# A transformer block with its gradients, rewritten: folded attention algebra, a token-major FFN in four column groups, transposes by DMA

## The chip, the core and the metric

The kernel runs on one core of a Trainium2 chip. A core has a matrix engine (TensorE, PE in the profile; loading its stationary operand is PEld), VectorE (DVE), ScalarE (ACT), GpSimd (POOL), a queue engine that only issues transfers (SP), and 16 DMA engines that all queues share. The engines run side by side and wait for each other through semaphores. The metric is the device time of one execution in microseconds, the median of several.

## The reference, cut to what matters

One block of a network with pre-layernorm, linear attention and a gated FFN, and the gradients of its output with respect to the input and the five weight matrices. S = 2048 tokens, D = 640 features, 32 heads of 20, F = 1728. Everything is bf16. `B_x` isn't used.

```python
def _A_ref(x, wqkv, wo):
    q, k, v = split_heads(x @ wqkv)
    phi = lambda t: jnp.where(t > 0, t + 1, jnp.exp(t)) + 1e-6
    pq, pk = phi(q), phi(k)
    kv = jnp.einsum("bhsd,bhse->bhde", pk, v)
    z = jnp.einsum("bhsd->bhd", pk)
    num = jnp.einsum("bhqd,bhde->bhqe", pq, kv)
    den = jnp.einsum("bhqd,bhd->bhq", pq, z)[..., None] + 1e-6
    return merge_heads(num / den) @ wo

def _B_ref(x, w_gate, w_up, w_down):
    g = _silu(x @ w_gate)
    u = x @ w_up
    return (g * u) @ w_down

h = x + _A_ref(_layernorm(x), A_wqkv, A_wo)
h2 = h + _B_ref(_layernorm(h), B_w_gate, B_w_up, B_w_down)
# outputs: h2, then the vjp of h2 at grad_out for A_x, A_wqkv, A_wo, B_w_gate, B_w_up, B_w_down
```

The attention has no softmax: all tokens share one 20x20 matrix kv per head and one vector z. In the gradients grad_out plays the part of dh2, the gradient to the FFN's input is turned into dh1 by the backward pass of the second layernorm and the residual, and dh1 goes back through the attention.

## The kernel before, in words

A matmul on TensorE contracts over the 128 partitions: `lhsT` is held still (128x128), `rhs` streams past column by column, and the result is summed in a PSUM bank of 512 fp32 columns. Which index lies on the partitions is therefore what a layout means here: token-major (`_tm`: 128 tokens on the partitions, 16 token tiles of 640 features) or feature-major (`T`: 128 features on the partitions, five tiles of 2048 tokens). A product that contracts over features needs feature-major operands, a weight gradient contracts over tokens and needs token-major ones, so most tensors are wanted in both. The kernel makes the second form on TensorE: `transpose_into` (lines 119 to 131) multiplies 128x128 blocks with an identity and copies groups of up to eight from PSUM to SBUF, by turns on VectorE (line 89) and ScalarE (line 91).

The stages, in the order of the text:

1. Lines 292 to 358. Layernorm of x (`bn_stats`, line 174; the norm, line 197), transposes to xnT, q feature-major (lines 310 to 317), k and v token-major (331 to 343), phi by exp and relu (236 to 240). grad_out is loaded and transposed (346 to 350), and so is wqkv (351 to 356).
2. Lines 363 to 415. kv as a block-diagonal matrix KVbd and its transpose, z, the denominators per token tile (389), their reciprocals spread over features by a small matmul (407), the numerators (411). The results are stored in DRAM.
3. Lines 420 to 434. Output projection plus residual (426, 428), second layernorm, transposes.
4. Lines 463 to 565, the FFN. The 1728 hidden features are cut into 14 tiles of 128 (the last has 64), in seven groups of two. Per hidden tile and chunk of 512 tokens: gate (494), up (498) and the gradient to the product, pdm = w_down dh2 (502), each five matmuls of 512 columns; ScalarE copies them out of PSUM (505 to 511) and VectorE forms m, du and dg (513 to 523). The three rows are stored feature-major in DRAM (524 to 526), transposed into token-major strips (528), and used for the gradients of w_down (552) and of w_gate and w_up (561).
5. Lines 609 to 631: h2 = h + m w_down (621), with m read back by token tile, and transposes of w_gate and w_up (599).
6. Lines 649 to 668: the gradient to the normalised h (663), and `ln_bwd_tile` (209 to 231), which gives dh1.
7. Lines 671 on: the attention backward. The gradient of wo (697), do (721), the denominators' gradient (731), dq (750), the gradients of kv (774, 779), dv and dk (803, 808), the gradient to xn and from it to x (837), the gradient of wqkv (856). Between them stand nine sets of transposes and several reloads from DRAM.

A planner places the instructions: it keeps each engine's list, takes the program's order as priority, and puts in semaphores and buffer waits. Tiles are drawn from pools; a tile with the same tag waits for a free buffer of its pool. The large tensors share a pool of six (`big`), 20 KB per partition each. SP issues most loads, POOL issues the stores and some loads, ACT a few.

Of the kernel before, what the change touches and what calls it, by code (L numbers as in the profile page):

```python
# [8 lines left out]
FP32 = mybir.dt.float32  # L9
BF16 = mybir.dt.bfloat16  # L10
ALU = mybir.AluOpType
# [5 lines left out]
DEBUG_OUT = {}  # L17
BIG_BUFS = 6
USE_BN_STATS = True
LN_MODE = "split"  # L20


class RR:

    def __init__(self, items):
        self.items = list(items)
        self.i = 0

    def __call__(self):
        it = self.items[self.i % len(self.items)]  # L30
        self.i += 1
        return it
# [3 lines left out]
def kernel(  # L36
    ctx, tc, A_x, A_wqkv, A_wo, B_x, B_w_gate, B_w_up, B_w_down, grad_out,
    out_0, out_1, out_2, out_3, out_4, out_5, out_6,
):
    nc = tc.nc  # L40
# [4 lines left out]
    SC = S // 512  # L45
    DT = D // P
    D3T = 3 * DT
    FT = (F + P - 1) // P
    fsz = [min(P, F - i * P) for i in range(FT)]
    NCH = [(i, min(i + 320, D)) for i in range(0, D, 320)]  # L50
    NW0 = NCH[0][1] - NCH[0][0]
    assert S % 512 == 0 and D % P == 0 and F % 64 == 0 and D % 320 == 0
    BIGSHAPE_TM = [P, ST, D]
    BIGSHAPE_FM = [P, DT, S]

    outs_list = [out_0, out_1, out_2, out_3, out_4, out_5, out_6]

    def dbg(name, ap, kind):
        if name not in DEBUG_OUT:
            return  # L60
        o = outs_list[DEBUG_OUT[name]]
        flat = o.rearrange("b s d -> (b s d)") if len(o.shape) == 3 else o.rearrange("a b -> (a b)")
        if kind == "tm":
            W = ap.shape[-1]
            v = flat[0:S * W].rearrange("(t p w) -> p t w", p=P, w=W)
        elif kind == "fm":
            J = ap.shape[1]
            v = flat[0:J * P * S].rearrange("(j p s) -> p j s", p=P, s=S)
# [10 lines left out]
    keep = ctx.enter_context(tc.tile_pool(name="keep", bufs=1))  # L79
    dram = ctx.enter_context(tc.tile_pool(name="dram", bufs=1, space=bass.MemoryType.DRAM))  # L80
    big = ctx.enter_context(tc.tile_pool(name="big", bufs=BIG_BUFS))

    dma_rr = RR([nc.sync, nc.gpsimd, nc.sync])
    evac_rr = RR(["v", "s"])

    def evac_copy(out, in_, eng=None):
        e = eng or evac_rr()
        if e == "v":
            nc.vector.tensor_copy(out=out, in_=in_)  # L89
        else:  # L90
            nc.scalar.copy(out=out, in_=in_)  # L91

    ident = const.tile([P, P], BF16, name="ident")
    make_identity(nc, ident[:])
    ones_bf = const.tile([P, H], BF16, name="ones_bf")
    nc.vector.memset(ones_bf[:], 1.0)
    eps6_col = const.tile([P, 1], FP32, name="eps6_col")
    nc.vector.memset(eps6_col[:], 1e-6)

    Efull = const.tile([P, D], BF16, name="Efull")  # L100
    nc.vector.memset(Efull[:], 0.0)
    E = Efull[:H, :]
    nc.gpsimd.memset(E, 1.0)
    nc.gpsimd.affine_select(out=E, in_=E, pattern=[[1, D]], compare_op=ALU.is_ge,
                            fill=0.0, base=0, channel_multiplier=-Dh)
    nc.gpsimd.affine_select(out=E, in_=E, pattern=[[-1, D]], compare_op=ALU.is_ge,
                            fill=0.0, base=Dh - 1, channel_multiplier=Dh)
    Mbd = const.tile([P, DT, D], BF16, name="Mbd")
    ET = const.tile([P, DT, H], BF16, name="ET")
# [6 lines left out]
    def tiles_overlapping(c0, c1):  # L116
        return [i for i in range(DT) if not (head_range(i)[1] <= c0 or head_range(i)[0] >= c1)]

    def transpose_into(dst_fn, src_fn, nblk, rows_in, ps_pool, tag="tr", cols_in=P, group=8, eng=None):
        b = 0  # L120
        group = max(1, min(group, (8 * P) // rows_in))
        while b < nblk:
            nb = min(group, nblk - b)
            pt = ps_pool.tile([P, 8 * P], BF16, name="pt_" + tag, tag=tag)
            for j in range(nb):
                src = src_fn(b + j)
                nc.tensor.transpose(out=pt[:cols_in, j * rows_in:(j + 1) * rows_in], in_=src,  # L127
                                    identity=ident[:rows_in, :rows_in])
            evac_copy(dst_fn(b, nb), pt[:cols_in, :nb * rows_in], eng)
            b += nb  # L130

    def tm_to_fm(dstT, src_tm, W, ps_pool, eng=None, tag="tr"):
        WT = W // P
        for j in range(WT):
            transpose_into(
                dst_fn=lambda b0, nb, j=j: dstT[:, j, b0 * P:(b0 + nb) * P],
                src_fn=lambda b, j=j: src_tm[:, b, j * P:(j + 1) * P],
                nblk=ST, rows_in=P, ps_pool=ps_pool, eng=eng, tag=tag)

    def fm_to_tm(dst_tm, srcT, W, ps_pool, eng=None, tag="tr"):  # L140
        WT = W // P
        for t in range(ST):
            transpose_into(
                dst_fn=lambda b0, nb, t=t: dst_tm[:, t, b0 * P:(b0 + nb) * P],
                src_fn=lambda b, t=t: srcT[:, b, t * P:(t + 1) * P],
                nblk=WT, rows_in=P, ps_pool=ps_pool, eng=eng, tag=tag)

    def layernorm_tiles(src_tm, dst_tm, mean, rstd, t0, nt, work, mode="bn"):
        mv = mean[:, t0:t0 + nt]
        rv = rstd[:, t0:t0 + nt]  # L150
        if mode == "act":
            ssum = work.tile([P, nt], FP32, name="ln_ssum", tag="ln_ssum")
            ssq = work.tile([P, nt], FP32, name="ln_ssq", tag="ln_ssq")
            for k in range(nt):
                t = t0 + k
                junk = work.tile([P, D], BF16, name="ln_junk", tag="ln_junk")
                nc.scalar.activation(out=junk[:], in_=src_tm[:, t, :], func=ACT.Copy, accum_out=ssum[:, k:k + 1])
                junk2 = work.tile([P, D], BF16, name="ln_junk2", tag="ln_junk")
                nc.scalar.activation(out=junk2[:], in_=src_tm[:, t, :], func=ACT.Square, accum_out=ssq[:, k:k + 1])
            nc.vector.tensor_scalar(out=mv, in0=ssum[:], scalar1=1.0 / D, scalar2=None, op0=ALU.mult)  # L160
            msq = work.tile([P, nt], FP32, name="ln_msq", tag="ln_msq")
            nc.vector.tensor_tensor(out=msq[:], in0=mv, in1=mv, op=ALU.mult)
            var = work.tile([P, nt], FP32, name="ln_var", tag="ln_var")
            nc.vector.scalar_tensor_tensor(out=var[:], in0=ssq[:], scalar=1.0 / D, in1=msq[:],
                                           op0=ALU.mult, op1=ALU.subtract)
            nc.vector.tensor_scalar(out=rv, in0=var[:], scalar1=1e-5, scalar2=None, op0=ALU.add)
        elif mode == "bn":
            a = len(NCH)
            mvv = work.tile([P, nt, 2], FP32, name="ln_mv", tag="ln_mv")
            for k in range(nt):  # L170
                t = t0 + k
                st6 = work.tile([P, a, 6], FP32, name="ln_st6", tag="ln_st6")
                for ci, (n0, n1) in enumerate(NCH):
                    nc.vector.bn_stats(out=st6[:, ci, :], in_=src_tm[:, t, n0:n1])
                nc.vector.bn_aggr(out=mvv[:, k, :], in_=st6[:].rearrange("p a b -> p (a b)"))
            nc.vector.tensor_copy(out=mv, in_=mvv[:, :, 0])
            nc.vector.tensor_scalar(out=rv, in0=mvv[:, :, 1], scalar1=1e-5, scalar2=None, op0=ALU.add)
        else:
            ssum = work.tile([P, nt], FP32, name="ln_ssum", tag="ln_ssum")
            ssq = work.tile([P, nt], FP32, name="ln_ssq", tag="ln_ssq")  # L180
            for k in range(nt):
                t = t0 + k
                nc.vector.tensor_reduce(out=ssum[:, k:k + 1], in_=src_tm[:, t, :], axis=AX.X, op=ALU.add)
                junk = work.tile([P, D], BF16, name="ln_junk", tag="ln_junk")
                nc.scalar.activation(out=junk[:], in_=src_tm[:, t, :], func=ACT.Square, accum_out=ssq[:, k:k + 1])
            nc.vector.tensor_scalar(out=mv, in0=ssum[:], scalar1=1.0 / D, scalar2=None, op0=ALU.mult)
            msq = work.tile([P, nt], FP32, name="ln_msq", tag="ln_msq")
            nc.vector.tensor_tensor(out=msq[:], in0=mv, in1=mv, op=ALU.mult)
            var = work.tile([P, nt], FP32, name="ln_var", tag="ln_var")
# [700 lines left out]
```

## Time and profile before

| | |
|---|---|
| three runs | 1111.87, 1112.3, 1115.91 us; median 1112.3 |
| the profiled execution | span 1114.9 us; no other time is given for it |
| TensorE | 1056.7 us busy, 95%, 8337 matmuls |
| VectorE, ScalarE, GpSimd | 571.8, 483.0, 133.4 us busy |
| DMA | 134.24 MB, mean 120 GB/s |
| mean granted TensorE clock | 0.981 |

How to read it: busy times are unions of the instructions' own intervals. Matmuls are pipelined, so the mean length of one (299 ns for 320 columns) is longer than the distance between two starts, and a busy PE isn't yet one at its peak. In a group's row stand the line, the engine, the operation, output and inputs by name, the shape, the count, then busy us and mean ns of one, then the idle time of the engine just ahead of it and who ended it. A DMA row ends with the size of one transfer and the median us from issue to landing.

### The profile page before, as it was taken

The numbers are of one execution on the slowest core, as the hardware profiler recorded it, in microseconds if no ns is written. First come the engines' busy times: TensorE is split into PE (matmuls) and PEld (weight loads), VectorE is DVE, ScalarE is ACT, GpSimd is POOL, SyncE is SP. The second block draws the span as 40 slices with busy tenths as digits, with TensorE's granted clock in tenths as the row PEclk, the third lists the DMA queues.
The fourth block names the chain that finished last, engine by engine and source line by source line (L and its number), as shares of the span: only waits on it lengthen the run. The fifth ranks groups of instructions, "written<-read, shape, count | busy, mean of one in ns | idle before, by whom it ended". The sixth has DMA issues, their size and how long they took to land.

```text
span 1114.9 us, 20384 instructions
## 1 busy us (share of the span) xinstructions
PE 1056.7 (95%) x8337; PEld 714.7 (64%) x8337; DVE 571.8 (51%) x1441; ACT 483.0 (43%) x951; POOL 133.4 (12%) x224
## 2 busy tenths in 40 slices
PE   5899998999999999999996999599989999899998
PEld 2477665575847576666756777377767467577775
DVE  8766676727273545545361232234343985477321
ACT  5755587526262535345351010122233686744231
POOL 2100000120202111111312013000000000011110
PEclk9899899999999999999999999799999999999999
DMA  8244364312222222212045954955440039411110
GB/s 318 75 138 150 159 247 146 125 61 86 92 82 96 78 103 78 98 41 107 31 159 182 219 136 139 298 119 122 100 153 31 1 123 351 181 39 43 42 36 30
DMA packets 134669, 134.24 MB, mean 120 GB/s; under 512 B 92384, under 2 KB 115680, under 8 KB 134320
## 3 DMA queue, kind: packets, MB, share of 16 engines
q0 software_dynamic: 20208, 77.58, 18.8%
q1 hardware_dynamic: 85440, 48.03, 15.4%
q10 hardware_dynamic: 28928, 7.34, 3.4%
q8 instruction: 65, 1.06, 0.4%
q14 instruction: 28, 0.23, 0.1%
HBM read 71.50 MB, written 61.42 MB: 119 GB/s over the span
## 4 chain that ended last, share of the span: by engine, by line
PE 69%; DMA 6%; DVE 6%; issue 1%; ACT 1%; POOL 0%; POOLq 0%; DVEq 0%; ACTq 0%; SPq 0%
PE accw L561 10%; PE acch L663 10%; PE acc_dxn L837 6%; PE accf L621 6%; PE acc_dwqkv L856 6%; PE pu L498 4%; PE pg L494 4%; PE acc L552 4%; PE pt_trs L127 4%; PE pt_tr L127 3%; PE pdm L502 3%; DMA dgcols<-scr_dgT 3%; PE acc_dwo L697 2%; PE ps_do L721 2%; DVE dm L519 1%
## 5 line engine op out<-in xcount | busy, mean ns | idle before, releaser
L561 PEld LDWEIGHTS <-hn_tm 128*128 128x128 bf16 x1120 | 107.1, 98 | 16.0 <-issue 4.8
L494 PE MATMUL pg<-hnT,wg_blk 128*128 128x512 bf16 (+1 forms) x280 | 76.2, 384 | 3.3 <-DMA wg_blk<-in_B_w_gate_dram 3.3
L663 PE MATMUL acch<-wgT,dgcols 128*128 128x320 bf16 x448 | 67.9, 304 | 12.0 <-DMA dgcols<-scr_dgT 11.5
L498 PE MATMUL pu<-hnT,wu_blk 128*128 128x512 bf16 (+1 forms) x280 | 74.7, 379 | 0.0
L89 DVE CAST dw_sb<-accw 128x256 bf16<-128x256 f32 (+1 forms) x35 | 14.5, 415 | 111.7 <-PE accw L561 86.8
L502 PE MATMUL pdm<-dh2T,wdT 128*128 128x512 bf16 (+1 forms) x280 | 69.6, 379 | 1.1 <-ACT dm L511 1.0
L552 PE MATMUL acc<-dh_tm,m_strip 128*128 128x320 bf16 (+1 forms) x448 | 69.3, 299 | 0.0
L621 PE MATMUL accf<-wd_big,mcols 128*128 128x320 bf16 x448 | 64.8, 306 | 3.6 <-DMA mcols<-scr_mT 3.6
L663 PE MATMUL acch<-wuT,ducols 128*128 128x320 bf16 x448 | 66.4, 300 | 0.0
L856 PE MATMUL acc_dwqkv<-cur_tm,xn_tmr 128*128 128x320 bf16 x480 | 65.7, 299 | 0.0
L663 PEld LDWEIGHTS <-dgcols 128*128 128x128 bf16 x448 | 44.4, 99 | 30.4 <-DMA dgcols<-scr_dgT 11.8
L561 PE MATMUL accw<-dg_strip,hn_tm 128*128 128x256 bf16 (+1 forms) x560 | 60.5, 269 | 3.4 <-ACT dw_sb L91 2.9
L561 PE MATMUL accw<-du_strip,hn_tm 128*128 128x256 bf16 (+1 forms) x560 | 60.3, 269 | 0.7 <-DVE dw_sb L89 0.7
L856 PEld LDWEIGHTS <-xn_tmr 128*128 128x128 bf16 x480 | 46.9, 98 | 18.1
L621 PEld LDWEIGHTS <-mcols 128*128 128x128 bf16 x448 | 44.0, 100 | 22.1 <-DMA mcols<-scr_mT 3.7
L91 ACT CAST dw_sb<-accw 128x256 bf16<-128x256 f32 (+1 forms) x35 | 12.8, 364 | 103.8 <-PE accw L561 98.9
L214 ACT ACTIVATE lb_dy<-acch 128x320 bf16<-128x320 f32 x32 | 14.0, 436 | 97.6 <-PE acch L663 97.6
L663 PEld LDWEIGHTS <-ducols 128*128 128x128 bf16 x448 | 44.0, 98 | 17.3
L552 PEld LDWEIGHTS <-m_strip 128*128 128x128 bf16 (+1 forms) x448 | 41.8, 99 | 13.5 <-issue 0.3
L229 DVE SCALAR_TENSOR_TENSOR lb_t<-lb_dy,lb_nm,lb_t 128x640 bf16<-128x640 bf16 x32 | 28.2, 880 | 41.1 <-ACT lb_t L227 41.1
L502 PEld LDWEIGHTS <-wdT 128*128 128x128 bf16 (+1 forms) x280 | 27.0, 98 | 34.4 <-DVE wdT L89 3.1
L565 POOL DMA_DIRECT2D out_dram<-dw_sb x70 | 37.7, 539 | 79.5 <-DVE dw_sb L89 44.9
(264 smaller groups left out, 2068.2 us busy)
## 6 DMA issues: line engine op xcount, KB each, us to landing
scr_mT<-mT_row POOLq DMA_DIRECT2D x14, 512.0 KB, 2.9
scr_duT<-duT_row POOLq DMA_DIRECT2D x14, 512.0 KB, 3.7
scr_dgT<-dgT_row POOLq DMA_DIRECT2D x14, 512.0 KB, 2.9
ducols<-scr_duT ACTq DMA_DIRECT2D x16, 448.0 KB, 4.7
mcols<-scr_mT SPq DMA_DIRECT2D x16, 448.0 KB, 4.1
dgcols<-scr_dgT SPq DMA_DIRECT2D x16, 448.0 KB, 4.2
out_dram<-dw_sb POOLq DMA_DIRECT2D x60, 64.0 KB, 1.8
x_tm<-in_A_x_dram SPq DMA_DIRECT2D x4, 640.0 KB, 6.3
```

The costliest lines, as they stand in the source:

```text
L127: nc.tensor.transpose(out=pt[:cols_in, j * rows_in:(j + 1) * rows_in], in_=src, identity=ident[:rows_in, :rows_in])
L229: nc.vector.scalar_tensor_tensor(out=t2[:], in0=dy[:], scalar=nm[:, 0:1], in1=t1[:], op0=ALU.subtract, op1=ALU.subtract)
L494: nc.tensor.matmul(pg[:fs, :], lhsT=wg_blk[:, kt, coff:coff + fs], rhs=hnT[:, kt, cs], start=(kt == 0), stop=(kt == DT - 1))
L498: nc.tensor.matmul(pu[:fs, :], lhsT=wu_blk[:, kt, coff:coff + fs], rhs=hnT[:, kt, cs], start=(kt == 0), stop=(kt == DT - 1))
L502: nc.tensor.matmul(pdm[:fs, :], lhsT=wdT_i[:, kt, :], rhs=dh2T[:, kt, cs], start=(kt == 0), stop=(kt == DT - 1))
L552: nc.tensor.matmul(acc[:fs, :w], lhsT=m_strip[:, t, coff:coff + fs], rhs=dh2_tm[:, t, n0:n1], start=(t == 0), stop=(t == ST - 1))
L561: nc.tensor.matmul(acc[:, :gw], lhsT=hn_tm[:, t, dt_ * P:(dt_ + 1) * P], rhs=strip[:, t, :gw], start=(t == 0), stop=(t == ST - 1))
L565: nc.gpsimd.dma_start(out=o_ap[dt_ * P:(dt_ + 1) * P, gcol0:gcol0 + gw], in_=dw_sb[:, :gw])
L621: nc.tensor.matmul(acc[:, :w], lhsT=mcols[:, j, :], rhs=wd_nat[:, j, n0:n1], start=(j == 0), stop=(j == FT - 1))
L663: nc.tensor.matmul(acc[:, :w], lhsT=cols[:, j, :], rhs=wT[:, j, n0:n1], start=(k == 0), stop=(k == 2 * FT - 1))
L837: nc.tensor.matmul(acc[:, :w], lhsT=srcT[:, jj, t * P:(t + 1) * P], rhs=wqkvT[:, j, n0:n1], start=(k == 0), stop=(k == D3T - 1))
L856: nc.tensor.matmul(acc[:, :w], lhsT=xn_tmr[:, t, dt_ * P:(dt_ + 1) * P], rhs=cur_tm[:, t, n0:n1], start=(t == 0), stop=(t == ST - 1))
```

## The change

The function is written anew; the reference, the inputs and the launch are the same. What it does:

**Algebra.** v, the numerators, o and do are no longer formed. With Y = xn^T pk (640x640), the matrix of all heads is kv^T = mask(wv^T Y), and W2 = kv wo; the attention's output is (pq/den) W2. Backward, dp = dh1 W2^T is the gradient to pq/den, GT = dh1^T (pq/den) stands for the gradient of wo (dwo = kv^T G) and of kv (mask(wo GT)), WV2 = dkv^T wv^T is the share of dv in the gradient to xn, and dwv = Y dkv. z is summed by a matmul with ones, which spreads it over all partitions, and the denominators are formed on VectorE.

**FFN, token-major.** Columns in four groups of 448, 448, 448 and 384. dm is computed ahead for all groups; then, per group, gate and up for two token tiles at a time, 896 wide; m, du and dg come out token-major and go into the weight gradients as they are. The gradient of w_down is formed as its transpose.

**Transposes by DMA.** Only xn is transposed on TensorE. All else uses a transposing DMA issued on SP: grad_out, the weights, pq/den, hn, every tile of dg and du (through a small tile `stg` to DRAM), m (read back from DRAM), dh1, and pk, dq and dk one tile at a time in a ring of three.

**Order.** Loops over token tiles run with a lag of one or two tiles, the down projection stands at the end, and the rstd is a power on GpSimd, not ScalarE's square root. The large pool has five buffers, a pool `strips` four.

The diff, of which the removed side is the listing above; the added side cut to its core:

```diff
+    def mm_row(ps, lhs, rhs, n, start=True, stop=True):
+        for ci, (n0, n1) in enumerate(NCH):
+            for k in range(n):
+                nc.tensor.matmul(ps[:, ci, :320], lhsT=lhs(k), rhs=rhs(k, n0, n1),
+                                 start=(start and k == 0), stop=(stop and k == n - 1))
...
+    for (t0, t1) in ((0, 1), (1, 2), (2, 4), (4, 6), (6, 8), (8, 10), (10, 12), (12, 14), (14, 16)):
...
+            tp = psum.tile([P, D], BF16, name="ps_t", tag="mm")
+            for kt in range(DT):
+                nc.tensor.transpose(tp[:, kt * P:(kt + 1) * P], xn[:, t, kt * P:(kt + 1) * P], ident[:])
+            nc.scalar.copy(out=xnT[:, :, t * P:(t + 1) * P], in_=tp[:].rearrange("p (k c) -> p k c", c=P))
+            for (dst, w0) in ((pk, D), (pqa, 0)):
+                ps = mm("ps_kq")
+                mm_row(ps, lambda k: xnT[:, k, t * P:(t + 1) * P], lambda k, n0, n1: wqk[:, k, w0 + n0:w0 + n1], DT)
+                nc.scalar.activation(out=e[:, :, :320], in_=row(ps), func=ACT.Exp)
+                nc.scalar.activation(out=r[:, :, :320], in_=row(ps), func=ACT.Relu)
...
+    for t in range(ST):
+        nc.vector.tensor_tensor(out=tz[:], in0=pq, in1=zb[:], op=ALU.mult)
+        nc.vector.tensor_reduce(out=den[:], in_=hb(tz[:]), axis=AX.X, op=ALU.add)
+        nc.vector.tensor_scalar(out=den[:], in0=den[:], scalar1=1e-6, scalar2=None, op0=ALU.add)
+        nc.vector.reciprocal(out=rall[:, t, :], in_=den[:])
+        nc.vector.tensor_tensor(out=hb(pqs[:]), in0=hb(pq), in1=bc(rall[:, t, :]), op=ALU.mult)
+        nc.sync.dma_start_transpose(out=pqsT[:, :, t * P:(t + 1) * P], in_=pqs[:])
...
+    for t in range(ST + 1):
+        if t < ST:
+            nc.sync.dma_start(out=xr[:], in_=x_v[:, t, :])
+            mm_row(ps, lambda i: pqsT[:, i, t * P:(t + 1) * P], lambda i, n0, n1: W2[:, i, n0:n1], DT)
+            nc.vector.tensor_tensor(out=half(xr[:]), in0=row(ps), in1=half(xr[:]), op=ALU.add)
+            ln_stats(xr[:], mv[:, 0, :])
+        u = t - 1
...
+        nc.sync.dma_start_transpose(out=hnT[:, :, u * P:(u + 1) * P], in_=hn[:, u, :])
...
+        for t in range(0, ST, 2):
+            nc.scalar.activation(out=dg, in_=pg[:, :, :w], func=ACT.Sigmoid)
+            nc.scalar.activation(out=nsg, in_=pg[:, :, :w], func=ACT.Sigmoid, scale=-1.0)
+            nc.scalar.copy(out=m, in_=pg[:, :, :w])
+            nc.scalar.copy(out=u, in_=pu[:, :, :w])
+            nc.vector.tensor_tensor(out=m, in0=m, in1=dg, op=ALU.mult)
+            nc.vector.tensor_tensor(out=nsg, in0=nsg, in1=m, op=ALU.mult)
+            nc.vector.tensor_tensor(out=nsg, in0=nsg, in1=dg, op=ALU.add)
+            nc.vector.tensor_tensor(out=du, in0=m, in1=dm, op=ALU.mult)
+            nc.vector.tensor_tensor(out=dg, in0=u, in1=dm, op=ALU.mult)
+            nc.vector.tensor_tensor(out=dg, in0=dg, in1=nsg, op=ALU.mult)
+            nc.vector.tensor_tensor(out=m, in0=m, in1=u, op=ALU.mult)
+            for c in range(2):
+                nc.sync.dma_start_transpose(out=stg[:, :GK[g], :], in_=ddt[:, tt + c, 0:2 * w])
+                nc.gpsimd.dma_start(out=scr_dT[t + c, :, KO[g]:KO[g] + GK[g], :], in_=stg[:, :GK[g], :])
...
+        if t < ST:
+            if t % 2 == 0 and t + 2 < ST:
+                load_cols(t // 2 + 1)
+            mm_row(ps, lambda k: cols[:, t % 2, k, :], lambda k, n0, n1: wgT[k // 14][:, k % 14, n0:n1], NKT)
+            ln_bwd(ps, hn[:, t, :], rstd2[:, t:t + 1], dh2[:, t, :], dh1[:, t, :], 0)
+            nc.sync.dma_start_transpose(out=dh1Ts[t], in_=dh1[:, t, :])
...
+    pqs_tm = big.tile([P, ST, D], BF16, name="pqs_tm", tag="B")
+    nc.sync.dma_start(out=pqs_tm[:], in_=scr_pqs_v)
...
+    for i in range(DT):
+        ps = mm("ps_gt")
+        mm_row(ps, lambda t: dh1[:, t, i * P:(i + 1) * P], lambda t, n0, n1: pqs_tm[:, t, n0:n1], ST)
...
+        if t < ST:
+            nc.sync.dma_start_transpose(out=pkT, in_=pkr[:])
+            nc.sync.dma_start_transpose(out=dqT, in_=dq[t // 8][:, t % 8, :])
+            mm_row(ps, lambda i: xtv[:, i, :], lambda i, n0, n1: WK2[:, i, n0:n1], DT)
+            nc.vector.tensor_tensor(out=dk[:, t, :], in0=tk[:], in1=pkr[:], op=ALU.mult)
+            nc.sync.dma_start_transpose(out=dkT, in_=dk[:, t, :])
...
+    for t in range(ST):
+        nc.sync.dma_start_transpose(out=mT[:, t % 4], in_=scr_m[t * P:(t + 1) * P, :])
+                nc.tensor.matmul(ps[:, ci, :320], lhsT=mT[:kk, t % 4, j, :], rhs=wd[:kk, j, n0:n1],
+                                 start=(j == 0), stop=(j == FT - 1))
```

More of the change, by code (lines that the diff above doesn't have):

```diff
@@ L16 @@
 H = 32
[L17 to L32, printed above, removed]
 @with_exitstack
@@ L93 @@
[L93 to L105, printed above, removed]
@@ L114, in head_range, with overlapping @@
         return Dh * h_lo, min(D, Dh * (h_hi + 1))
-    def tiles_overlapping(c0, c1):
+    def overlapping(c0, c1):
         return [i for i in range(DT) if not (head_range(i)[1] <= c0 or head_range(i)[0] >= c1)]
[L119 to L146, printed above, removed]
@@ new lines @@
+    nc.gpsimd.dma_start(out=mat_v(scr_dKVT), in_=dKVT[:])
+    wvk = strips.tile([P, 2, DT, D], BF16, name="wvk", tag="S")
+    WV2 = wvk[:, 0]
+    WK2 = wvk[:, 1]
+    for i in range(DT):
+        js = overlapping(i * P, (i + 1) * P)
+        ps = mm("ps_wv2")
+        mm_row(ps, lambda k: dKVT[:, js[k], i * P:(i + 1) * P], lambda k, n0, n1: wqkvT[:, 10 + js[k], n0:n1], len(js))
+        nc.scalar.copy(out=half(WV2[:, i, :]), in_=row(ps))
+        nc.sync.dma_start_transpose(out=WK2[:, :, i * P:(i + 1) * P], in_=WV2[:, i, :])
```

1140 lines of the change are left out of this document (432 added, 708 removed).

## The prediction

> **What bounds the kernel now.** I read the page first, then a few stretches, then the PE timeline, then the waits.
>
> ```profile
> span 1114.9 us, 20384 instructions
> PE 1056.7 (95%) x8337; PEld 714.7 (64%) x8337; DVE 571.8 (51%) x1441; ACT 483.0 (43%) x951; POOL 133.4 (12%) x224
> ...
> PE   5899998999999999999996999599989999899998
> ...
> PEclk9899899999999999999999999799999999999999
> ...
> PE 69%; DMA 6%; DVE 6%; issue 1%; ACT 1%; POOL 0%; POOLq 0%; DVEq 0%; ACTq 0%; SPq 0%
> ```
>
> TensorE is busy 95% of the span, and 69% of the chain that ended last is its own. The windows show whether that busy time is dense (columns: window, its length, then busy time and count of PE, PEld, DVE, ACT, POOL; granted clock, DMA share, GB/s):
>
> ```profile
> 0.00:25.00 25.00, 13.18 (x83) 7.13 (x84) 21.61 (x75) 14.35 (x21) 7.86 (x13) 1.00 0.92 328
> 700.00:725.00 25.00, 13.55 (x86) 8.90 (x84) 5.92 (x14) 3.12 (x8) 0.87 (x1) 0.73 1.17 291
> 875.00:900.00 25.00, 24.41 (x110) 10.53 (x109) 24.54 (x77) 16.28 (x31) 0.00 (x0) 1.00 0.00 1
> 975.00:1000.00 25.00, 25.00 (x187) 18.01 (x185) 17.81 (x43) 11.08 (x32) 2.74 (x5) 1.00 0.12 43
> ```
>
> Around 975 PE starts 187 matmuls in 25 us at full clock; around 875 VectorE is as full as PE, with 110; at 0 and at 700 PE waits. The timeline gives the rate and the cost of a transpose (start, length, engine, line):
>
> ```profile
> 258.09 0.61 PE L127 MATMUL pt_trs<-ident,mT_row 128*128 128x128 bf16 x8
> ...
> 258.54 1.03 PE L494 MATMUL pg<-hnT,wg_blk 128*128 128x512 bf16 x4
> ...
> 974.73 0.84 PE L837 MATMUL acc_dxn<-wqkvT,dqTr 128*128 128x320 bf16 x5
> 975.41 0.84 PE L837 MATMUL acc_dxn<-wqkvT,dkT 128*128 128x320 bf16 x5
> ```
>
> Five matmuls of 320 columns every 0.68 us: 0.136 us each, **0.425 ns per column** of the moving operand. Eight transposes of 128 columns take 0.45 us, about the same per column. So the work of PE can be summed in columns. These rows show a second thing: line 494 belongs to the next hidden tile, and stands in the program after all the strip transposes of this one, yet its matmuls run between them. Instructions are placed by readiness, not by the order of the text; an engine's gap can be filled from further on.
>
> ```profile
> PE pt_tr L127 <- DVE xn_tm L197: 13.7, 2, 11.0
> PE acch L663 <- DMA dgcols<-scr_dgT: 11.5, 1, 11.5
> ```
>
> (waiter, releaser: us in all, times, longest.) The two long waits are the start and a column load early in the gradient to hn.
>
> **The sum of the old kernel, as a test of the method.** Thousands of columns, from the loop bounds and tile widths in the listing: transposes 251 (1,963 of them), q/k/v, KV, den, num and output projection 283, gate/up/dm 430, FFN weight gradients 420, down projection 143, gradient to hn 287, attention backward 550. Together 2,364 thousand x 0.425 ns = 1,005 us. The span is 1,114.9, so 110 us are not columns: 58 idle (1,114.9 - 1,056.7) and 52 inside the busy share, where VectorE sets the pace or the clock falls. The page gives this execution no time beside its span; it stands 2.6 us above the 1,112.3 median and within the three runs, so I predict without a correction.
>
> **The change, part by part: PE.** After, in thousands of columns: 80 transposes for xn, 10 (the other 1,883 go to the DMA); k and q 102; z 10; Y = xnT pk 51; masks, KVT, dKVT 8; W2 and WV2 17; x + pqs W2 51; gate/up/dm token-major 415 (no padding of the last tile); FFN weight gradients 415; gradient to hn 276; dp 51; GT 51; dz 11; dk 51; dxn 154; dwq and dwk 102; dwo and dwv, folded, 18; down projection 143. Sum 1,938 thousand x 0.425 = **824 us**: 181 less, of which transposes are 102 (241 x 0.425) and the algebra with the padding 79.
>
> **Other engines, per stage.**
>
> ```profile
> L625 DVE TENSOR_TENSOR h2t<-accf,h_tm 128x320 bf16<-128x320 f32 x32 | 15.6, 491 | 51.0 <-PE accf L621 47.6 <-DMA out_dram<-h2t 3.5
> L514 DVE TENSOR_TENSOR mT_row<-gp,u_bf 128x512 bf16<-128x512 bf16 x52 | 21.8, 419 | 2.4 <-ACT u_bf L509 1.0
> L240 DVE TENSOR_TENSOR pk_tm<-phi_e,phi_r 128x320 bf16<-128x320 bf16 x32 | 10.1, 315 | 0.1
> L174 DVE BATCH_NORM_STATS2 ln_st<-x_tm 128x6 f32<-128x320 bf16 x32 | 13.6, 458 | 2.2 <-DMA x_tm<-in_A_x_dram 2.2
> L183 DVE TENSOR_REDUCE ln_ssum<-h_tm 128x1 f32<-128x640 bf16 x16 | 13.1, 816 | 6.9 <-ACT h_tm L430 6.9
> L197 DVE TENSOR_SCALAR hn_tm<-h_tm,mean,rstd 128x640 bf16<-128x640 bf16 x16 | 6.1, 442 | 0.1
> L393 DVE RECIPROCAL dsm<-dsm 128x32 f32<-128x32 f32 x16 | 5.1, 344 | 1.2 <-ACT dsm L392 0.9
> L243 DVE TENSOR_SCALAR phk<-pkT 128x512 bf16<-128x512 bf16 x20 | 5.7, 292 | 0.6
> L91 ACT COPY wqkvT_a<-pt_tr 128x896 bf16<-128x896 bf16 x5 | 4.5, 905 | 3.2 <-PE pt_tr L127 3.2
> L91 ACT COPY o_tm<-pt_tr 128x640 bf16<-128x640 bf16 x8 | 5.2, 694 | 3.6 <-PE pt_tr L127 3.6
> ```
>
> - First stage, per token tile: ACT makes five passes of 640 (694 ns): 3.5 us, 56 us for 16 tiles; VectorE two statistics, a norm, four phi passes: 3.1 us; PE 0.27 + 20 x 0.136 = 3.0 us. ACT sets the pace, by 8 us over PE; dm matmuls can fill. I put 6.
> - Denominators (per tile a product, a reduce, reciprocal, two small, a broadcast product with an fp32 column, which I place between 490 and 816 ns, near the upper): 2.6 us, 42 in all; residual plus statistics plus norm 0.82 + 0.92 + 0.19 + 0.44 = 2.4 us, 38 in all. With 50 of the first stage VectorE has 130 us up to hnT, PE (Y, W2, the projection and the 59 us of dm included) 161. If dm fills the gaps, nothing is added; if it doesn't, PE idles about 16 + 20 us.
> - Gate/up, per two tiles: PE 20 x 448 x 0.425 = 3.8 us; ACT four passes of 896, 3.6; VectorE seven products, (419-315)/192 = 0.54 ns an element, so 627 ns each, 4.4 us. **VectorE is the slowest here**, 35 us a group against PE's 30; the following weight gradients give PE 46 us in which VectorE has three copies. All four strip buffers belong to one group, so the next group can't run far ahead. Uncovered, a group loses about 7 us (lead-in 2.7, pace 4.6); covered, none. I take 3, 12 in all.
> - Gradient to hn and dp: PE 64 x 0.136 = 8.7 us a tile, VectorE some twelve passes, 6.5: hidden. dk and dxn: PE 5.4, VectorE 3.6, ACT 1.5: hidden.
>
> **DMA.** Plain traffic, from shapes, 117 MB (before 134 by the page). New: 219 transposing DMAs on SP's queue, 1,739 blocks of 128x128, 57 MB. No trace shows one.
>
> ```profile
> q0 software_dynamic: 20208, 77.58, 18.8%
> ...
> q10 hardware_dynamic: 28928, 7.34, 3.4%
> ...
> xr<-in_A_x_dram SPq DMA_DIRECT2D x16, 160.0 KB, 8.7
> ...
> xn_tmr<-scr_xn_tm SPq DMA_DIRECT2D x1, 2560.0 KB, 11.9
> ...
> wd_i<-in_B_w_down_dram SPq DMA_DIRECT2D x13, 160.0 KB, 2.4
> ...
> wqkv<-in_A_wqkv_dram SPq DMA_DIRECT2D x1, 800.0 KB, 9.5
> ```
>
> Queue 0 moves 77.58 MB in 18.8% of 1,114.9 us (370 GB/s when it moves), queue 10, whose pieces are 256 bytes, 194. A 160 KB tile, then, costs 0.44 to 0.84 us if transposes stream; 2.4 us if each is waited out; 8.7, the worst landing of such a tile, at the far end. I take 0.84, as a transpose moves short pieces: 294 us of transposes and 316 of plain traffic, 610 of some 890. It is hidden then, by PE.
>
> One page speaks against this. The Trainium skill, page "VectorE: DVE Perf Modes", section "The three transpose paths", puts a 128x128 bf16 transpose at 1309 ns by the DMA and 390 ns on TensorE. The trace gives TensorE's as 56 ns in a row (0.45 us for eight), so that figure is an isolated latency; no run here shows the DMA's. By it, if blocks don't overlap, an estimate is 6.5 us a tile and 2.3 ms for all, far slower than before; the rival below is that mechanism from rows.
>
> **Fixed parts.** Start 9 us (800 KB of weights landed after 9.5, in a busier start). Entry to the gradient to hn, 3: its first column load can go early into the strip that dm leaves. Entry to GT: the 2.6 MB of pqs_tm wait for a buffer that the last hn matmul frees, 11.9 us less three dp tiles (4.1), so 8. WV2, its transposes, then dk: 4, as dwq can fill. End: add and store, 4. And 16 us for the excess inside busy time: 52 before, of which the stretches with rows of transposes and VectorE's pace in the old attention backward fall away. The old waits of 11.0 and 11.5 us go with their stages; what is late next is the GT load.
>
> Sum: 824 + 6 + 12 + 9 + 3 + 8 + 4 + 4 + 16 = **886 us**.
>
> **Rivals.**
> 1. *The placing doesn't fill.* Readiness is judged ahead of the run, with the new DMAs in every chain (pqs to pqsT to projection to hn to hnT). In the order of the text a residual load would stand behind the transpose of the tile before: 2.4 + 2.4 + 0.8 = 5.6 us (load, VectorE, transpose) a tile against PE's 1.4, +67; the first stage's copy-matmul-exp chain 5.2 against 3.5, +27; FFN uncovered, +17. Of these 111 us about two thirds: 960. For it: waits on loads exist (11.5). Against: the interleaving above.
> 2. *Everything fills.* Start, end and GT alone remain: 824 + 9 + 8 + 4 = 845. Against: the old kernel leaves 110 us.
> 3. *Slower: the transposes set the pace of one queue.* At c us per 160 KB: dk/dxn has three per tile, so 16 x (3c - 5.4); a FFN group 22.4c against 76; the down projection 16 tiles x 2.8c against 108 us of cover (dwq, dwk, dwo, itself); denominators 16 x (c - 2.6). At 2.4 only the first counts, +29: 915. It decides from c = 3.9 (+101, +45, +67, +21). At c = 5: +154, +143, +116, +38, so 1,340 us. For it: 160 KB have taken 8.7 us. Against: that was behind megabytes of loads, and nothing in the rows says that a stream must be waited out.
> 4. *The folding is not what it says*: the columns are counted from the loops, so this is small; within 1 it would show as more matmuls.
>
> **How the numbers follow.** Forecast 0.60 (own range 850 to 925: FFN and entries at their ends, and c up to 2.4), rival 1 0.20 (925 to 1,010), rival 2 0.10 (835 to 850), rival 3 0.10, of which a tenth lands between 1,010 and 1,118. About 0.5% is what a measurement of this kernel tells from no change. Faster: 0.60 + 0.20 + 0.10 + a little of rival 3 = 0.90; the same 0.01; slower 0.09. Range: 840 leaves out some 0.05, 1,010 some 0.10.
>
> **What would show it.** Right: PE's groups of 448 columns start 0.19 us apart, some 5,460 matmuls; PE busy about 860; VectorE at nine tenths in four gate/up stretches; PE's waits on DMA under 30 us. Wrong: PE waiting for pqsT, dkT or mT; SP's queue full; PE starting below 187 matmuls of 320 per 25 us in dxn; dm running after hnT instead of within.

## The result, and the profile after

The changed kernel takes 1001.7 us (median of five; 998.7 to 1013.2) against 1115.9 for the kernel before, measured beside it: ratio 0.899, 95% interval 0.894 to 0.904. It is faster, by 114 us where 226 were forecast, and inside the range. The profiled execution is the slowest of the five, 1013.2 us with a span of 1011.5.

The changed kernel's page (busy times, PE and its granted clock in 40 slices, one DMA queue, the chain):

```profile
span 1011.5 us, 14023 instructions
...
PE 859.4 (85%) x5461; PEld 533.6 (53%) x5461; DVE 425.0 (42%) x889; ACT 299.2 (30%) x421; POOL 253.1 (25%) x430
...
PE   2667956999999999999999199997948777997996
...
PEclk9999979999999999999999699998978999998998
...
q1 hardware_dynamic: 251312, 79.36, 43.1%
...
PE 54%; DVE 15%; DMA 13%; issue 6%; SPq 5%; ACT 3%; POOL 2%; POOLq 0%; DVEq 0%; ACTq 0%
```

PE's work is what was forecast: 5,461 matmuls and 859 us busy ("some 5,460", "about 860"). But PE stands still for 152 us where the old kernel left 58, at the start, around slice 22 and from slice 27 on. The waits of PE name the places (waiter, releaser: us in all, times, longest):

```profile
PE ps_dp L117 <- DMA dh1T<-dh: 26.8, 2, 20.4
PE ps_kq L117 <- ACT xnT L214: 26.2, 16, 1.7
PE ps_dk L117 <- DMA xt<-scr_xnT: 18.8, 10, 2.7
PE ps_a L117 <- DVE xr L299: 17.1, 7, 9.7
PE ps_t L213 <- DVE xn L209: 17.0, 1, 17.0
PE ps_dxn L550 <- DMA ring<-dk: 13.8, 3, 9.0
```

Stage by stage, from the first and last start of each group of matmuls. The forecast column is the prediction's columns times 0.425 ns plus the extra that it gave that stage; the last column is the fastest kernel below, e15_all.

| stretch | forecast | after | e15_all |
|---|---|---|---|
| start to the first matmul | 9 | 17 | 17 |
| first stage (transposes of xn, k, q) | 54 | 79 | 51 |
| z, Y, W2, projection, dm | 112 | 139 | 115 |
| gate/up and weight gradients | 306 | 300 | 308 |
| gradient to hn, dp | 142 | 170 | 156 |
| GT to the first dk | 44 | 38 | 38 |
| dk and dxn | 87 | 132 | 98 |
| dwq, dwk, dwo | 47 | 56 | 56 |
| down projection, dwv | 65 | 72 | 72 |
| end | 4 | 9 | 9 |
| excess, spread | 16 | | |
| sum | 886 | 1012 | 919 |

(Rounded line by line.)

The FFN stretch (gate/up and weight gradients), a third of PE's columns, came out 2% under the forecast. Most of the gap lies in four stretches: the first stage, the one that dm was to fill, the entry to dp, and dk/dxn.

### The profile page after: what moved, and what is told of

Read it like the earlier page. It is cut to its first block, busy times and chain, and to the rows that moved or that the text cites. A ratio compares the mean times of both kernels' runs of the same rounds, so it can differ in the third digit from the quotient of the medians.

```text
span 1011.5 us, 14023 instructions
## 1 busy us (share of the span) xinstructions
PE 859.4 (85%) x5461; PEld 533.6 (53%) x5461; DVE 425.0 (42%) x889; ACT 299.2 (30%) x421; POOL 253.1 (25%) x430
## 3 DMA queue, kind: packets, MB, share of 16 engines
q1 hardware_dynamic: 251312, 79.36, 43.1%
## 4 chain that ended last, share of the span: by engine, by line
PE 54%; DVE 15%; DMA 13%; issue 6%; SPq 5%; ACT 3%; POOL 2%; POOLq 0%; DVEq 0%; ACTq 0%
PE ps_dw L400 16%; PE ps_dhn L117 10%; PE ps_dm L321 6%; PE ps_kq L117 5%; PE ps_dxn L550 3%; PE ps_o L599 3%; DMA ring<-pkr 2%; PE ps_dp L117 2%; DMA dh1T<-dh 2%; PE ps_gt L117 2%; SPq L592 2%; DMA xt<-scr_xnT 2%; PE pg L357 2%; DVE m_s L383 1%; DVE m_s L377 1%
## 5 line engine op out<-in xcount | busy, mean ns | idle before, releaser
L400 PE MATMUL ps_dw<-dd,hn 128*128 128x448 bf16 (+1 forms) x640 | 119.9, 346 | 7.0 <-DVE dd L382 6.9
L117 PE MATMUL ps_dhn<-wgT,cols 128*128 128x320 bf16 x864 | 120.8, 301 | 0.0
L117 PEld LDWEIGHTS <-cols 128*128 128x128 bf16 x864 | 85.1, 98 | 33.8
L400 PEld LDWEIGHTS <-hn 128*128 128x128 bf16 x640 | 62.6, 98 | 62.3 <-issue 8.7
L599 PE MATMUL ps_o<-wd,mT 128*128 128x320 bf16 x448 | 67.7, 300 | 0.0
L550 PE MATMUL ps_dxn<-wqkvT,ring 128*128 128x320 bf16 x320 | 55.8, 318 | 13.8 <-DMA ring<-dk 13.8
L362 PE MATMUL pu<-wgu,hnT 128*128 128x448 bf16 (+1 forms) x320 | 63.6, 346 | 0.0
L357 PE MATMUL pg<-wgu,hnT 128*128 128x448 bf16 (+1 forms) x320 | 63.6, 346 | 0.0
L400 PE MATMUL ps_dw<-m_s,dh 128*128 128x448 bf16 (+1 forms) x320 | 60.4, 346 | 0.0
L321 PE MATMUL ps_dm<-wdT,dh2T 128*128 128x448 bf16 (+1 forms) x320 | 58.6, 346 | 0.8 <-DVE xr L299 0.8
L117 PE MATMUL ps_dp<-W2T,dh1T 128*128 128x320 bf16 x160 | 26.8, 320 | 26.8 <-DMA dh1T<-dh 26.8
L117 PE MATMUL ps_dk<-wvk,xt 128*128 128x320 bf16 x160 | 28.1, 332 | 23.2 <-DMA xt<-scr_xnT 18.8
```

What stands on the lines that cost most here:

```text
L117: nc.tensor.matmul(ps[:, ci, :320], lhsT=lhs(k), rhs=rhs(k, n0, n1), start=(start and k == 0), stop=(stop and k == n - 1))
L321: nc.tensor.matmul(ps[:, c, :w], lhsT=dh2T[:, kt, (t + c) * P:(t + c + 1) * P], rhs=wdT[g // 2][:, kt, o:o + w], start=(kt == 0), stop=(kt ...
L357: nc.tensor.matmul(pg[:, c, :w], lhsT=hnT[:, kt, (t + c) * P:(t + c + 1) * P], rhs=wg[:, kt, 0:w], start=(kt == 0), stop=(kt == DT - 1))
L362: nc.tensor.matmul(pu[:, c, :w], lhsT=hnT[:, kt, (t + c) * P:(t + c + 1) * P], rhs=wg[:, kt, w:2 * w], start=(kt == 0), stop=(kt == DT - 1))
L400: nc.tensor.matmul(ps[:, c, :w], lhsT=lhs(t), rhs=rhs(t), start=(t == 0), stop=(t == ST - 1))
L550: nc.tensor.matmul(ps[:, ci, :320], lhsT=lhs[:, i, :], rhs=rhs[:, i, n0:n1], start=(k == 0 and i == 0), stop=(k == 2 and i == DT - 1))
```

## The experiments

Each line of a diff is against the changed kernel, or against the kernel that its expectation names; `...` stands for what is left out. Each ratio is to the kernel before, run beside the experiment. "After" is the changed kernel, 0.899.

**Does dm fill?** In the changed kernel all 320 dm matmuls run after the projection. All its PSUM tiles carry one tag with four buffers; the old kernel had several pools.

e1_dm_pool:

```diff
-psum ... bufs=4
+psum ... bufs=3
+psum2 ... bufs=1
-            ps = mm("ps_dm")
+            ps = psum2.tile([P, 2, 512], FP32, name="ps_dm", tag="dm")
```

> The dm products get a PSUM pool of their own (one tile of two banks; the other tag keeps three). Theory A, that one shared PSUM tag holds the matmuls in the order of the text: dm now stands between the first stage's and the projection's matmuls, fills PE's gaps of the first 176 us (about 55 us of them), and the kernel takes 950 to 975 us against 1001.7. Rival B, that dm was held back because grad_out's transposes come late: dm moves too, but PE then waits for dh2T near the start, some 20 us, so 975 to 990, with a new wait of PE for that transpose. Rival C, that the planner does not fill at all: dm stays behind the projection and the time stays within 5 us.

1036.8 us, ratio 0.930 (0.926 to 0.935): slower than after. The tile view of ps_dm, and PE's waits, both of e1_dm_pool:

```profile
L322 PE MATMUL ps_dm<-wdT,dh2T x320: 322/352/581, 30.0 to 259.8; 128*128 128x448 bf16 x120, 128*128 128x384 bf16 x40
```

```profile
PE ps_dm L322 <- ACT dme L328: 15.1, 16, 1.0
...
PE pg L358 <- DMA wgu<-in_B_w_gate_dram: 14.3, 1, 14.3
...
PE ps_dm L322 <- DMA dh2T<-in_grad_out_dram: 12.5, 1, 12.5
```

With a pool of its own dm runs from 30 us on, so the shared tag had held it behind everything ahead of it in the text. But the planner placed it as if dh2T came sooner than it did: PE stood for 12.5 us until 30 us. The gate weights then waited for a buffer that dm still held. So this edit cost more than it saved. It doesn't give the worth of filling, because it also takes buffers away: dm's single buffer makes PE wait 15.1 us for ACT's copies, and all other matmuls have three buffers instead of four.

e3_dm_text: dm keeps the shared tag, but its 32 units are put by hand.

```diff
+    dm_next(8)
     W2 = big.tile(...)
...
+            dm_next()
             ps = mm("ps_a")
```

> The shared tag stays; the text is changed: eight dm units stand ahead of W2, one ahead of each projection tile, eight behind. Theory A: PE follows the text, so the 45 us of the moved units cover the idle time of the stretch from 125 to 176 us, about 20 us; 978 to 988 us. Rival: the stretch is paced by transfers on SP's queue and not by VectorE, then the moved matmuls only push the chain back: above 995.

985.7 us, ratio 0.883 (0.880 to 0.886), and the FFN begins at 211.8 us instead of 234.8. PE's wait for the adds (L299 in after, 17.1 us) is gone from the list.

**The first stage.** One tile of after shows its chain (start, length, engine):

```profile
64.39 2.89 PE L117 MATMUL ps_kq<-wqk,xnT 128*128 128x320 bf16 x20 [1.70 <-ACT xnT L214]
65.95 0.70 ACT L220 ACTIVATE phi_e<-ps_kq 128x640 bf16<-128x640 f32 x1 [1.62 <-PE ps_kq L117]
66.55 0.70 ACT L221 ACTIVATE phi_r<-ps_kq 128x640 bf16<-128x640 f32 x1
67.11 0.44 PE L213 MATMUL ps_t<-ident,xn 128*128 128x128 bf16 x5
67.31 0.70 ACT L220 ACTIVATE phi_e<-ps_kq 128x640 bf16<-128x640 f32 x1
67.91 0.70 ACT L221 ACTIVATE phi_r<-ps_kq 128x640 bf16<-128x640 f32 x1
68.50 0.70 ACT L214 COPY xnT<-ps_t 128x640 bf16<-128x640 bf16 x1
69.25 0.58 PE L117 MATMUL ps_kq<-wqk,xnT 128*128 128x320 bf16 x3 [1.70 <-ACT xnT L214]
```

The copy of the next xnT stands on ACT behind the exponentials of this tile, and PE waits 1.7 us for it: 4.86 us a tile, neither engine full. e4_lag1 puts transposes and copy one tile ahead:

```diff
+            if t > 0:
+                kq(t - 1)
+    kq(ST - 1)
```

> In the first stage the transpose and copy of tile t+1 stand ahead of the k and q products of tile t. Theory: the stage's 4.9 us a tile is the chain copy, k product, exp, relu on ScalarE's queue; with the copy ahead it falls to ScalarE's own 3.5 us, 15 tiles x 1.3 = 20 us less: 978 to 986. Rival: the stage is slowed by the transfers of 0 to 75 us (DMA share near 1), then 997 to 1003.

989.0 us, 0.886 (0.881 to 0.892). z starts at 67.9 us instead of 96.3: 3.2 us a tile, under the 3.5 of the forecast. But the FFN starts only 15 us earlier: ps_kvt now waits 12.9 us for VectorE, which is still at the denominators and itself waits 10.6 us for pqsT's transposes.

**The entry to dp.** e5_gate_wo holds woT's transpose, which stood ahead of dh1T on SP's queue, until dh1 is complete. What SP issues there in after (start, length):

```profile
549.19 9.99 SPq L485 DMA_TRANSPOSE woT<-in_A_wo_dram  x1
559.24 14.33 SPq L455 DMA_TRANSPOSE dh1T<-dh  x2
```

```diff
+    nc.vector.tensor_copy(out=woT[:, 0, 0:1], in_=dh1[:, ST - 1, 0:1])
```

> The transpose of wo is kept back until dh1 is complete (one column of its tile is first written from the last dh1 tile). Theory: PE's 20 us wait for the first dh1 transpose was the transpose of wo ahead of it in SP's queue (10 us of issue, 27.7 to landing); without it the wait falls to 3 to 8 us: 984 to 992. Rival: W2's transpose, which waits for a freed pool, sets that wait alone: 998 or more. The time of wo's transpose then lies under GT.

1001.3 us, 0.896 (0.895 to 0.898): no difference. The dp waits were 13.9 us there against 26.8 in after's profile, but 12 to 20 in kernels that leave this stretch alone, so the 26.8 belongs to after's profiled execution, the slowest of the five. There the first dh1T took 18.0 us from issue to landing. In e8_gate_start, which leaves this stretch alone, it took 2.6 us behind 9.3 us of woT's issue; in e5_gate_wo, with woT out of the way, 13.1. What the queue gave back, the transfer took, and what slows the transfer wasn't tried. Neither was W2T, whose transpose waits 8.9 us for the stores of dwev. The cause of this wait stays open.

**dk and dxn.** A tile takes 7.75 us where PE's own work is 5.4. One turn of after (SPq: what SP issues):

```profile
789.55 0.49 DVE L540 TENSOR_TENSOR dk<-tk,pkr 128x640 bf16<-128x640 bf16 x1
...
790.12 1.20 SPq L541 DMA_TRANSPOSE ring<-dk  x1
...
791.26 0.55 POOL L554 DMA_DIRECT2D out_dram<-dx  x1 [6.96 <-DVE dx L142]
791.37 1.30 SPq L534 DMA_TRANSPOSE ring<-dq  x1
...
791.80 0.54 POOL L530 DMA_DIRECT2D xt<-scr_xnT  x1
...
792.78 1.25 SPq L533 DMA_TRANSPOSE ring<-pkr  x1
795.38 1.53 PE L117 MATMUL ps_dk<-wvk,xt 128*128 128x320 bf16 x10 [2.13 <-DMA xt<-scr_xnT]
796.41 0.33 DVE L535 TENSOR_SCALAR pkr<-pkr 128x640 bf16<-128x640 bf16 x1 [4.70 <-DMA ring<-pkr]
...
797.58 0.49 DVE L540 TENSOR_TENSOR dk<-tk,pkr 128x640 bf16<-128x640 bf16 x1
```

PE's wait names xt, whose load stands on POOL behind the dx store. VectorE's names pkr: the clamp (L535) overwrites pkr, so it waits until the transpose has read it, and that one is third on SP. Four runs take these apart. e6_gate_gky holds back the transposes of G, KV and Y, which had gone ahead of dkT(0):

```diff
     G = mat("G")
+    nc.vector.tensor_copy(out=G[:, 0, 0:1], in_=dk[:, ST - 1, 0:1])
...
```

> The transposed loads of G, KV and Y are held back by one-element copies until the last dk tile is there, so that they no longer stand ahead of dkT(0) on SP's queue at the start of the dk/dxn stage. Theory (these loads are what the first dxn tile waits for; in the changed kernel's profile they were issued at 743.6 to 756.3 us, ahead of dkT(0), with 9.0 and 3.3 us of waits behind): the stage's start is 10 to 13 us shorter, 988 to 992 us. Rival (the three loads only move, and ps_o or dwqk then wait for them, or the loop's pace takes it over): 998 us or more.

997.6 us, 0.894 (0.892 to 0.896), an interval that meets after's. PE's wait on the ring falls from 13.8 to 5.8 us, that on dwo rises from 7.3 to 11.9: between theory and rival.

e7_dx_act:

```diff
-        nc.gpsimd.dma_start(out=o1_v[:, u, :], in_=dx[:])
+        nc.scalar.dma_start(out=o1_v[:, u, :], in_=dx[:])
```

> The store of dx (L554) goes out on ACT's queue instead of POOL's; nothing else is changed, and the order of the matmuls is the same. Theory (the dk/dxn loop runs at 7.75 us a tile because the next xt load stands behind the dx store on POOL's queue, and PE's 18.8 us of waits on xt in this stage come from there): the pace falls towards PE's 5.4 us, 20 to 30 us less in all, 972 to 982 us. Rival (the buffers of xt, or the transposes on SP, set the pace): 998 us or more.

1008.3 us, 0.904 (0.903 to 0.906): the rival. PE's waits on xt are gone; in their place it waits 28.6 us for the ring and 10.0 for ACT. The wait that the view named wasn't the cause.

e11_clamp:

```diff
+            pkc = wk("pkc", pool=1)
-            nc.vector.tensor_scalar(out=pkr[:], in0=pkr[:], ...)
+            nc.vector.tensor_scalar(out=pkc[:], in0=pkr[:], ...)
...
-            nc.vector.tensor_tensor(out=dk[:, t, :], in0=tk[:], in1=pkr[:], op=ALU.mult)
+            nc.vector.tensor_tensor(out=dk[:, t, :], in0=tk[:], in1=pkc[:], op=ALU.mult)
```

> In the dk/dxn loop the clamp of pkr (L535) writes a tile of its own instead of pkr in place, so that VectorE no longer waits for pkr's transpose; the dx store stays on POOL's queue. Theory (two cycles of about equal length hold this loop, 8.0 us by dk, dkT, dqT and pkrT in SP's order, clamp, dk, and about 8 us by dx, the dx store, the xt load behind it on POOL, ps_dk, dk, dx): with one of them cut the other remains, 996 us or more. Rival (pkr's transpose alone sets the pace): 20 to 30 us less, 972 to 982 us.

972.8 us, 0.872 (0.869 to 0.875): 29 us less. My theory of two equal cycles fell, and the rival holds. In e11_clamp's timeline:

```profile
780.50 0.32 DVE L536 TENSOR_SCALAR pkc<-pkr 128x640 bf16<-128x640 bf16 x1
...
781.20 1.52 PE L117 MATMUL ps_dk<-wvk,xt 128*128 128x320 bf16 x10
...
786.63 1.52 PE L117 MATMUL ps_dk<-wvk,xt 128*128 128x320 bf16 x10
```

5.43 us a tile, the forecast's 5.4, with the same three transposes a tile. VectorE makes dx after dk in its order, so the dx store and the xt load behind it come earlier once dk does; that is read from the two timelines, not tried alone.

e12_clamp_dx, both edits:

> Both edits of the dk/dxn loop at once: the clamp of pkr in a tile of its own, and the dx store on ACT's queue. Theory (the two cycles of equal length are all that holds the loop above PE's 5.4 us a tile): the pace falls from 7.75 to between 5.5 and 6.3 us, 20 to 35 us less in all, 967 to 982 us, where each edit alone gave nothing. Rival (the transposes themselves, some 1.3 us of issue each on SP and 0.5 of the DMA engines' time, set the pace): 995 us or more.

973.8 us, 0.873 (0.869 to 0.877): the same as e11_clamp. Moving the store to ACT's queue brought nothing, alone or with the clamp freed.

**The start.** e8_gate_start holds the transposes of dh2 and Wd behind tiles 3 to 10 by one-element copies as in e6_gate_gky.

> The transposed loads of dh2 and Wd, which the changed kernel issues at the very start on SP (wdT(0) at 4.8, dh2T at 15.1 to 59 us), are held back by one-element copies behind tiles 3 to 10 of the first stage. Theory (at the start they take the DMA engines that the first x tile needs; PE's first matmul came at 17.0 us against 9 forecast): the first matmul comes at 10 to 12 us, 994 to 997 us in all. Rival (the 17 us are the first x tile's own path, and dh2T now arrives too late for dm): no change or slower, 1,000 us or more.

1003.0 us, 0.898 (0.896 to 0.901); the first matmul still comes at 16.6 us. The rival: the transposes don't hold up the start. After's first norm (L209) stands on VectorE behind the statistics of further tiles, which wait for their loads until 11.6 us, and the rstd that it needs is begun on POOL only at 13.5 us, behind the same tiles' steps. That is read from after's timeline; no run tried another order.

**Do the gains add?** e9_lag1_dm is e4 and e3 together:

> Both orders at once: the first stage's transposes and copy one tile ahead of its matmuls (as in e4_lag1), and the dm units put by the text, 8 before W2, 16 among the projection's tiles, 8 after it (as in e3_dm_text). Theory (up to the FFN the time is PE's order in the text, and the two gains are of different stretches): the FFN starts at about 185 us instead of 234.8, 952 to 973 us in all (973 if the two totals just add). Rival (the dm units run into dh2T's and wdT's late loads, or VectorE, with the projection's adds, sets the stretch): the FFN starts at 205 us or later, 980 us or more.

984.4 us, 0.881 (0.877 to 0.884): no more than e3 alone. The FFN starts at 206.6 us, and PE and VectorE wait thus in e9_lag1_dm:

```profile
PE ps_kvt L307 <- DVE yk L309: 24.9, 1, 24.9
```

```profile
DVE pqs L290 <- DMA pqsT<-pqs: 22.3, 1, 22.3
```

Two causes were possible. e13_xnT_early sends each xnT store right behind its copy, since pqsT takes xnT's buffer:

> The kernel of e9_lag1_dm, with each store of a block of xnT put right behind its copy instead of four at a time behind the stores of xn, pk and pq. Theory (pqsT takes the buffer of xnT, so that it waits for the last of these stores; in e9_lag1_dm's chain they stood at 71.4 and 87.5 us with 15.3 and 12.6 us, VectorE then waited 22.3 us for pqsT's transposes, and PE 24.9 us for VectorE): PE's wait at ps_kvt falls below 10 us, 966 to 975 us in all. Rival (the DMA engines are full until about 100 us, and the transposes of dh2 and Wd, not the order of the stores, set when pqsT can be written): the wait stays at 20 us or more, 980 us or more.

The four executions took 985.3, 989.5, 984.6 and 965.8 us. The first is the profiled one, and its wait at ps_kvt is still 25.4 us: so far the rival. The last lies just under the theory's range, and no trace shows why. What SP issues in e13_xnT_early (start, length):

```profile
14.88 38.33 SPq L192 DMA_TRANSPOSE dh2T<-in_grad_out_dram  x4
53.25 44.14 SPq L188 DMA_TRANSPOSE wdT<-in_B_w_down_dram  x3
98.13 27.52 SPq L291 DMA_TRANSPOSE pqsT<-pqs  x10
```

SP's queue is taken until 97.4 us, and pqsT follows at once. In e9_lag1_dm the queue was free at 89.4 us, and pqsT came at 100.4: SP waited 10.7 us for the stores of xnT. In e13_xnT_early that wait is 0.4 us, but the three transposes of Wd take 44 us instead of 33. So there were two waits, one behind the other. e14_wd_late keeps the early stores and holds the three back:

```diff
-    for g in range(1, 4):
-        load_wdT(g)
...
+        if t in (3, 7, 11):
+            g = t // 4 + 1
+            nc.vector.tensor_copy(out=wdT[g // 2][:, 0, ...], in_=tz[:, 0:1])
+            load_wdT(g)
```

> The kernel of e13_xnT_early, with the transposed loads of Wd's second to fourth column group held behind the normalised queries of tiles 3, 7 and 11. In e13_xnT_early these three held SP's queue from 53.3 to 97.4 us, and pqsT's transposes stood behind them. Theory (that is what VectorE's wait of 22.9 us for pqsT, and through it PE's 25.4 us at ps_kvt, came from): PE's wait at ps_kvt falls to 10 us or less, 963 to 974 us. Rival (the DMA engines are full to about 100 us whatever the order, or the granted clock, 0.949 against 0.967 in e3_dm_text, takes back what PE no longer waits): 979 us or more.

965.1 us, 0.866 (0.863 to 0.868), and in its list of PE's waits:

```profile
PE ps_kvt L308 <- DVE yk L310: 2.7, 1, 2.7
```

The wait falls as the theory says, and the time is 19 us below e9_lag1_dm's. That is the gain of both edits. How much the second brings alone isn't shown: one execution of e13_xnT_early was as fast without it, and it wasn't run without the early stores. In after the same three transposes were issued within 12 us, by 71 us, and pqsT was first issued at 104.5: the wait came with the faster first stage. Why the three then take longer wasn't tried.

e15_all joins what helped:

> All that helped so far: the kernel of e14_wd_late, with the clamp of pkr in a tile of its own (e11_clamp, 29 us less) and G, KV and Y gated (e6_gate_gky, 4 us less). Theory (these stretches don't overlap, so the gains add): 33 us less than e14_wd_late, 930 to 942 us. Rival (the gains overlap, or the granted clock falls further as PE waits less): 950 us or more.

921.7 us, 0.826 (0.824 to 0.828): 43 us less than e14_wd_late, more than the two gains apart, and faster than the kernel before and after. The dk/dxn stretch alone gives 38 of them (136 us in e14_wd_late, 98 here). Its page:

```profile
span 919.1 us, 14072 instructions
...
PE 846.2 (92%) x5461; PEld 530.9 (58%) x5461; DVE 428.7 (47%) x895; ACT 297.2 (32%) x421; POOL 250.7 (27%) x430
```

e16_all_kvt moves eight dm units once more:

> The kernel of e15_all, with the first 8 dm units put ahead of the matmuls of ps_kvt instead of behind them. Theory (these 16 us of PE work cover VectorE's denominators, for which ps_kvt's evacuation waits): 4 to 8 us less than e15_all. Rival (VectorE's adds in the projection are then the next wait, or dm waits for dh2T): within 2 us of e15_all.

933.4 us, 0.837 (0.834 to 0.839): slower, and outside both expectations. The wait at ps_kvt rose from 2.4 to 4.3 us, the FFN began 3.8 us later, dp waited 4.5 longer; the rest is spread, and why I leave open.

## Why the prediction was wrong

- **The sum of columns was right.** PE's count and busy time, the FFN (300 for 306; of the 12 us put for VectorE's pace, PE waited 6.9), GT to dk (38 for 44), and dk/dxn at 5.43 us a tile once freed. "Folding isn't what it says" falls. (Two slips changed nothing: the terms as printed add to 1,936 thousand, not 1,938, which is 1 us; and the 8.7 us called the worst landing of a tile is a group's median.)
- **"If dm fills the gaps, nothing is added" failed**, and with it the step that carried it, "instructions are placed by readiness, not by the order of the text". The old kernel's rows were read rightly, and after's planner, too, departs from the text in places (the first norm at the start). But the new kernel has one PSUM tag for all, and all 320 dm matmuls stayed behind the projection (from 176.4 us). e1_dm_pool shows the tag's part: with a pool of their own they begin at 30.0 us. e3_dm_text shows what filling by hand is worth: 16 us. That the tag's buffers go round in text order, and that the old kernel's several pools let line 494 through, is argued. This was rival 1's mechanism, and the time lies in rival 1's range; its "residual load behind the transpose" is there too (9.7 us of the wait on L299), its FFN share isn't.
- **First stage: "ACT sets the pace", 3.5 us, was mis-sized**: 4.86, near rival 1's 5.2. I had summed ACT's passes and not followed the copy's place in ACT's order. e4_lag1 brings 3.2, less than the sum, as the passes are 0.70 us long but start 0.60 apart.
- **dk/dxn "hidden" failed**, 45 us, the largest miss. PE, VectorE and ACT were costed as loads on an engine; the loop was closed through a tile overwritten in place: dk, dkT, dqT, pkrT, clamp, dk. e11_clamp shows it.
- **The transposes' size was right, their use wasn't.** Queue 1, plain loads included, moved 79.36 MB in 43.1% of 1011.5 us: 0.90 us per 160 KB beside the 0.84 taken. Rival 3 falls as a pace. But a transpose has 1.2 us of issue on SP, and pkr's came 3.6 us after its issue; in a closed chain that counts, not the throughput. The landing of dk's tile of five blocks in after (KB left out, median us):

```profile
ring<-dk SPq DMA_TRANSPOSE x8, 2.6
```

  The Trainium skill, page "VectorE: DVE Perf Modes", section "The three transpose paths", gives 1309 ns for one 128x128 block by the DMA. By it, five blocks one behind the other would take an estimated 6.5 us. These rows do not agree with that: five land in 2.6 us from their issue, 0.52 a block, and in the stream five take 0.90 us, 0.18 a block. No run has a single block alone.
- **Entry to dp, 3 us, failed**: 12 to 27. I looked at the first column load and forgot that dp needs W2T and dh1T on SP's queue. Which of the two, or the transfer itself, sets the wait is open. GT's 8 was too much.
- **Start 9 and end 4** were 17 and 9.

Three of the prediction's own signs spoke against it in after's profile: dm ran after the projection; PE started 152 matmuls in the 25 us from 775 us, below 187 (186 in e11_clamp); and its waits on DMA came to 64 us, over the 30.

Of the 126 us between the forecast and the profiled span of after, e15_all recovers 92.

## What to carry over

A stage's pace isn't the largest of its engines' sums until the order on each queue and each in-place write has been followed round the loop once: write down who frees what, as carefully as who computes what. Matmuls that are to fill gaps got there by a place in the text (e3_dm_text); a PSUM pool of their own moved them too, but not to a good place (e1_dm_pool). And the gain of one stage can hide behind the next queue until that is moved too.

## What the runs showed of the hardware

The longest wait named isn't always the cause: PE waited 18.8 us for xt, and an edit to pkr brought that to 3.3. And a pause costs beyond its length. Windows of after around the 20 us wait at dp (length, busy and count of PE, PEld, DVE, ACT, POOL, granted clock, DMA share, GB/s):

```profile
570.00:577.00 7.00, 0.00 (x0) 0.00 (x0) 0.00 (x0) 0.00 (x0) 0.00 (x0) 0.50 1.12 210
...
580.00:581.00 1.00, 1.00 (x6) 0.52 (x5) 0.00 (x0) 0.64 (x2) 0.00 (x0) 0.50 0.00 0
...
583.00:584.00 1.00, 1.00 (x9) 0.73 (x8) 1.00 (x3) 0.00 (x0) 0.00 (x0) 1.00 0.00 0
```

PE stops at 557.1 us, and the granted clock falls to 0.50 at about 562. PE restarts at 577.5 us with the clock at 0.50 and has it back at about 582.5. The Trainium skill, page "TensorE: Matmul & The Clock Gate", section "The HAM clock gate", has the clock at half after an idle window of about 3.4 us and back after as long a busy one; the trace agrees in kind, with about 5 us each way. In e15_all, which pauses less, the same 5,461 matmuls take 846 us of busy time instead of 859, at a mean granted clock of 0.978 instead of 0.958.

Large transposes out of DRAM vary widely in the time that they take of SP's queue. Four of 640 KB at the start took 31 (e4_lag1) to 44 us (after). Three of Wd took 12 us in after, 33 in e9_lag1_dm and 44 in e13_xnT_early, though the DMA share was about 1.2 in all three. What sets this wasn't tried.
